# A one-core kernel of attention and two MoE layers: block 0 of the first layer in two halves around block 1

## The chip, the cores and the metric

The kernel runs on one core of a Trainium2 chip. The metric is the device time of one execution in microseconds (us); lower is better. Engines are named as in the profile: PE is TensorE (PEld its weight loads), DVE is VectorE, ACT is ScalarE, POOL is GpSimd, SP issues most DMAs. L546 is line 546 of the kernel before.

## The reference

```python
# q, k, v: (4, 8, 768, 64); sinks 4, window 128; x: 3072 tokens x 512
scores = np.where(is_sink | in_window, scale * q @ k.T, -1e9)
attn_out = softmax(scores) @ v
x = attn_out.transpose(0, 2, 1, 3).reshape(3072, 512)
h = np.maximum(x @ w_in, 0.0)          # w_in: 512 x 2048
x = (h * h) @ w_out                    # w_out: 2048 x 512
logits = x @ w_gate                    # 8 experts, the largest logit's one is taken
# for the tokens of each expert e:
h = np.maximum(x[mask] @ w1[e], 0.0)   # w1[e]: 512 x 1024
out[mask] = gate_w * eom[e] * (h @ w2[e])
```

Everything is fp32 in the reference. The kernel splits fp32 numbers into a high and a low half that PE takes (fp32r) and adds three products.

## The kernel before

The 3072 tokens are worked in 12 blocks of 256 (`NBLK`). Attention of block t writes its 256 tokens, transposed, into the one tile `xr`; `split_x(t)` (L507) then splits `xr` into `xT`, high and low halves, four pieces of 256 columns, the high half on ACT (L512) and the low half on DVE (L513). Each of the four needs its own part of `xr`; the branch in front of it (L509) is taken only for inputs of another kind.

The first layer of a block runs in 16 slices of the hidden width (`NF`). For slice j, `l1(t, j)` (L540) multiplies `xT` by `WI[j]` (12 matmuls of 256 columns, L546), takes the relu on ACT (L549), squares on DVE (L550; in block 0 every second slice on POOL), and splits the result into `h2` (ACT L552, DVE L553). `l2(t, j)` (L556) runs two slices later and adds `h2` times `WO[j]` (6 matmuls of 512 columns, L562) to two PSUM accumulators, psx0 and psx1. After slice 15 they are copied to a tile (L570 on ACT, L572 on DVE), from which `gate_pieces` (L584) works out the second layer's routing in four steps and stores the block to `x2tab` in DRAM.

The weights `WI` and `WO` arrive in 32 pieces of 512 KB (`conv`, L261): piece 2j is `WI[j]`, piece 2j + 1 is `WO[j]`. A piece is loaded into one of the three buffers of the ring `stage`, changed on ACT (L275, L276), put together on DVE by two shifts (L278, L279), cast into the high half (DVE L283, every third one ACT L281), and POOL subtracts to get the low half (L284). The main loop (L909 on) calls `cstep` in block 0 so that before slice j the pieces up to 17 + j are done in program order; 13 stand before slice 0.

The order of everything is made by a scheduler from the program's order and priorities, and each engine works its list in that order. Attention of block t is a list of timed events (`attn_events`, L515): two slots a slice, eight tiles (four pairs of heads, two halves of 128 queries), with `prep_k`, `prep_q`, `scores`, `ptrans`, `pv` at the leads of `LEADS`. In the kernel before the tiles of a block come every four slots, that is every two slices, so that attention of block t spreads over the 16 slices of block t - 1 and some of the block ahead. The last steps, `fin_sink` and `add_sink`, add the four sink tokens to `xr`. Blocks 0 and 1 do attention in plain fp32 (`T32`): a score tile is two matmuls in the program and four passes in the trace (L400), a product L472. From block 2 on they are split as the first layer is (L404, L479).

```python
            cstep(max(2 * j + 3, 17 + j) - st_["done"])
```

Of the kernel before, what the change touches and what calls it, by code (L numbers as in the profile page):

```python
# [30 lines left out]
XW = 513  # L31
# [3 lines left out]
LEADS = ((5, 2, 4.5, 8.5), (5, 2, 4.5, 8), (5.5, 2.5, 4.5, 8))  # L35
# [7 lines left out]
def kern(ctx, tc, q, k, v, n_sink, window, w_in, w_out, w_gate, w_og, w1, w2, out):  # L43
# [15 lines left out]
    xtab = dram.tile([B * H, D, S], F32, name="xtab")  # L59

# [446 lines left out]
    def split_x(t):  # L507
        b, u = divmod(t, NQ // 2)
        with tc.If(gv > 0):  # L509
            SY.dma_start(out=xr[:], in_=xtab[H * b:H * b + H, :, 256 * u:256 * u + 256].rearrange("(p e) d s -> (e d) p s", e=2))  # L510
        for kk in range(4):
            A.activation(out=xT[:, 0, kk], in_=xr[:, kk], func=AF.Copy)  # L512
            V.tensor_tensor(out=xT[:, 1, kk], in0=xr[:, kk], in1=xT[:, 0, kk].bitcast(F32), op=ALU.subtract)  # L513

    def attn_events(t):  # L515

        ev = []
        h0 = 32 * (t - 1) - 8
        a0, a1, a2, a3 = LEADS[min(t, 2)]
        for p in range(4):  # L520
            ev.append((h0 + 8 * p - a0, lambda p=p: prep_k(t, p)))
            ev.append((h0 + 8 * p - a1, lambda p=p: prep_q(t, p)))
        for n in range(8):
            ev.append((h0 + 4 * n, lambda n=n: scores(t, n // 2, n % 2)))
            ev.append((h0 + 4 * n + a2, lambda n=n: ptrans(t, n // 2, n % 2)))
            ev.append((h0 + 4 * n + a3, lambda n=n: pv(t, n // 2, n % 2)))
        if t % 3 == 0:
            ev.append((h0 + 31, lambda: prep_sink(t // 3)))
        else:
            ev.append((h0 + 31, lambda: fin_sink(t)))  # L530
# [9 lines left out]
    def l1(t, j):  # L540
# [9 lines left out]
        (G if t == 0 and j % 2 else V).tensor_tensor(out=hq[:], in0=hq[:], in1=hq[:], op=ALU.mult)  # L550
# [4 lines left out]

    def l2(t, j):  # L556
        if j == 0:
            acc[t] = [psX.tile([128, 512], F32, tag=f"x{m}", name=f"psx{m}") for m in range(2)]
        o = h2.pop((t, j))
        for m in range(2):  # L560
            for n, (a_, b_) in enumerate(((0, 0), (0, 1), (1, 0))):
                PE.matmul(acc[t][m][:], lhsT=o[:, a_, 128 * m:128 * m + 128], rhs=WO[j // 8][:, j % 8, b_, :],  # L562
                          start=(j == 0 and n == 0), stop=(j == NF - 1 and n == 2))
        if j == NF - 1:
            xs = []
            both = cv.tile([128, 2, XW], F32, tag="stage", name="x2s", bufs=3)
            for m in range(2):
                x = both[:, m]
                if m == 0:
# [338 lines left out]
    G2 = NBLK * NF  # L908
    for g in range(G2):  # L909
        t, j = divmod(g, NF)  # L910
# [20 lines left out]
        if t == 0:  # L931
            cstep(max(2 * j + 3, 17 + j) - st_["done"])
        with (tc.high_priority(20) if t == 0 else ExitStack()):
            swap = t > 0 and j == 0
            if swap:
                l2(*divmod(g - 2, NF))
# [3 lines left out]
            if j == NF - 1 and t + 1 < NBLK:  # L940
                split_x(t + 1)
            if swap:
                l1(t, j)
            elif g >= 2:
                l2(*divmod(g - 2, NF))
            if g >= 2:
                if j == 1 and t > 0:
                    gate_events(t - 1)
# [150 lines left out]
```

## Time and profile before

| | |
|---|---|
| runs | 1193.41 us median of 3 (1192.56 to 1198.88) |
| the profiled execution | 1196.3 us, its span 1194.5 us |
| PE busy | 1138.7 us (95% of the span) |
| DVE, ACT, POOL busy | 761.5, 626.5, 457.9 us |
| first layer's first l1 matmul | 59.50 us |

A row of a timeline gives its start, how long it lasted, engine, line, operation, what it writes and reads, how many instructions it merges, and in brackets the idle time of the engine before it with what ended that. A row of lines gives a group's count, its busy time and the mean length of one instruction, then the engine's idle time before its instructions. Granted clock is given as a share of 2.4 GHz; where no record of the clock lies in a stretch, it reads 1.00.

### The profile page before, as it was taken

What the parts mean: (1) busy time and instruction counts of PE and PEld (TensorE: products, weight loads), DVE (VectorE), ACT (ScalarE), POOL (GpSimd) and SP (SyncE); (2) the same over time, 40 slices, a digit from 0 to 9 for tenths busy, and PEclk for the clock granted to TensorE, in tenths of its full rate; (3) what the DMA queues carried; (4) which work ended last, traced back from release to release, by engine and by line L of the source; (5) the groups of instructions that cost most, each with busy time, mean ns of one, the idle gap of its engine ahead of it and who ended that gap; (6) DMA issues with size and microseconds to landing.
All of it is one profiled execution on the core that took longest, in us unless ns stands there. A gap on an engine that the chain in (4) does not pass through costs nothing. (4 is left out here: it accounts for less than half of the span.)

```text
span 1194.5 us, 24037 instructions
## 1 busy us (share of the span) xinstructions
PE 1138.7 (95%) x7022; PEld 945.7 (79%) x7022; DVE 761.5 (64%) x2123; ACT 626.5 (52%) x1740; POOL 457.9 (38%) x949
## 2 busy tenths in 40 slices
PE   4898889999999999999999999999899999999996
PEld 2476678888888888888888888887788888888884
DVE  4699776767676667676767677656611466764153
ACT  3677576767666766666676666545222222222200
POOL 4256665326565335555424556310211222222111
PEclk9999899999999999999999999999999999999998
DMA  4565411111211211121112120087411357554110
GB/s 123 132 181 176 137 35 45 32 51 37 54 32 28 50 37 46 35 49 29 47 35 51 37 54 1 19 182 207 133 39 44 100 179 255 189 203 151 42 51 23
DMA packets 139387, 100.08 MB, mean 84 GB/s; under 512 B 103903, under 2 KB 112223, under 8 KB 139234
## 3 DMA queue, kind: packets, MB, share of 16 engines
q1 hardware_dynamic: 132674, 83.85, 25.1%
q0 software_dynamic: 5472, 14.19, 3.6%
q8 instruction: 64, 1.05, 0.4%
q14 instruction: 89, 0.73, 0.3%
q10 hardware_dynamic: 1088, 0.26, 0.1%
HBM read 85.56 MB, written 13.76 MB: 83 GB/s over the span
## 5 line engine op out<-in xcount | busy, mean ns | idle before, releaser
L546 PE MATMUL psh<-xT,WI 128*128 128x256 f32 x2304 | 314.8, 285 | 10.6 <-POOL WI L284 8.1
L546 PEld LDWEIGHTS psh<-xT,WI 128*128 128x128 f32 x2304 | 294.9, 190 | 29.0 <-POOL WI L284 10.9
L867 PE MATMUL psh<-WI,xt 128*128 (+1 forms) x672 | 164.8, 400 | 0.3 <-ACT ht L847 0.3
L562 PE MATMUL psx<-WOb,h 128*128 128x512 f32 x576 | 157.8, 410 | 2.7 <-ACT h L552 2.4
L562 PE MATMUL psx<-WOa,h 128*128 128x512 f32 x576 | 159.0, 409 | 0.0
L867 PEld LDWEIGHTS psh<-WI,xt 128*128 128x128 f32 x672 | 124.3, 188 | 27.9 <-ACT xt L847 0.5
L550 DVE TENSOR_TENSOR r<-r 128x256 f32<-128x256 f32 x184 | 83.6, 455 | 68.3 <-ACT r L549 66.7
L562 PEld LDWEIGHTS psx<-WOb,h 128*128 128x128 f32 x576 | 102.6, 191 | 23.4 <-ACT h L552 3.9
L412 ACT ACTIVATE P<-P,st 128x260 f32<-128x260 f32 (+1 forms) x192 | 92.7, 485 | 47.4 <-DVE st L410 45.1
L883 DVE TENSOR_TENSOR ht<-psht,ht 128x512 fp32r<-128x512 f32 x56 | 38.5, 689 | 123.9 <-ACT ht L847 123.5
L549 ACT ACTIVATE r<-psh 128x256 f32<-128x256 f32 x192 | 72.2, 377 | 83.6 <-PE psh L546 72.4
L562 PEld LDWEIGHTS psx<-WOa,h 128*128 128x128 f32 x576 | 102.1, 190 | 17.4 <-issue 0.3
L553 DVE TENSOR_TENSOR h<-r,h 128x256 fp32r<-128x256 f32 x192 | 91.9, 479 | 29.3 <-ACT h L552 25.7
L905 POOL DMA_INDIRECT out_dram<-xg,pidx x28 | 31.2, 1116 | 193.5 <-ACT xg L904 152.0
L408 DVE CUSTOM_DVE_ANT_0 P<-pss,M 128x260 f32<-128x260 f32 (+1 forms) x184 | 72.5, 403 | 28.2 <-PE pss L404 14.3
L455 POOL TENSOR_SCALAR_AFFINE_SELECT PT<-PT 128x256 fp32r<-128x256 f32 x224 | 85.1, 415 | 12.9 <-DVE st L410 12.8
L552 ACT ACTIVATE h<-r 128x256 fp32r<-128x256 f32 x192 | 78.1, 408 | 22.2 <-DVE r L550 18.0
L896 PE MATMUL psy<-WOb,ht 128*128 (+1 forms) x336 | 85.1, 402 | 0.0
L896 PE MATMUL psy<-WOa,ht 128*128 (+1 forms) x336 | 84.1, 397 | 0.0
L873 ACT ACTIVATE r<-psh 128x512 f32<-128x512 f32 x48 | 28.7, 598 | 99.7 <-PE psh L867 97.8
L838 POOL DMA_INDIRECT xg<-x2tab,pidx x30 | 40.7, 1356 | 95.5 <-issue 55.9
L489 POOL TENSOR_TENSOR xr<-tB,tC 128x128 f32<-128x128 f32 x80 | 37.6, 470 | 97.8 <-DVE tB L488 95.3
(430 smaller groups left out, 1979.3 us busy)
## 6 DMA issues: line engine op xcount, KB each, us to landing
raw<-in_moe_w_dram SPq DMA_DIRECT2D x36, 1024.0 KB, 6.2
craw<-in_moe_w_in_dram SPq DMA_DIRECT2D x16, 512.0 KB, 3.8
craw<-in_moe_w_out_dram SPq DMA_DIRECT2D x16, 512.0 KB, 3.2
x2tab<-x2s SPq DMA_DIRECT2D x24, 256.5 KB, 3.1
kn<-in_k_dram SPq DMA_DIRECT2D x64, 96.0 KB, 2.3
vn<-in_v_dram SPq DMA_DIRECT2D x64, 96.0 KB, 2.2
qn<-in_q_dram SPq DMA_DIRECT2D x92, 64.0 KB, 2.1
kn<-in_k_dram SPq DMA_DIRECT2D x32, 64.0 KB, 2.1
```

The source lines that it names most:

```text
L408: V.tensor_tensor_reduce(out=P[:, e, 0:W], in0=ps[e][:, 0:W], in1=mask[:, 0:W], scale=1.0, scalar=-3.0e38, op0=ALU.add, op1=ALU.max, accum ...
L412: A.activation(out=P[:, e, 0:W], in_=P[:, e, 0:W], func=AF.Exp, scale=SCALE, bias=st[:, 2 + e:3 + e], accum_out=st[:, 4 + e:5 + e])
L455: G.affine_select(out=both[:, 1 - b, e], in_=bf[:, 0, e], pattern=[[0, 2], [1 - 2 * b, 128]], compare_op=ALU.is_gt if b else ALU.is_ge, fi ...
L546: PE.matmul(ps[:], lhsT=WI[:, j, a_, kk, :], rhs=x[:, b_, kk, :], start=(n == 0), stop=(n == 11))
L549: A.activation(out=hq[:], in_=ps[:], func=AF.Relu)
L550: (G if t == 0 and j % 2 else V).tensor_tensor(out=hq[:], in0=hq[:], in1=hq[:], op=ALU.mult)
L552: A.activation(out=o[:, 0], in_=hq[:], func=AF.Copy)
L553: V.tensor_tensor(out=o[:, 1], in0=hq[:], in1=o[:, 0].bitcast(F32), op=ALU.subtract)
L562: PE.matmul(acc[t][m][:], lhsT=o[:, a_, 128 * m:128 * m + 128], rhs=WO[j // 8][:, j % 8, b_, :], start=(j == 0 and n == 0), stop=(j == NF ...
L838: G.indirect_dma_start(out=x, out_offset=None, in_=x2tab[:] if s >= PRE else x2tab[0:256 * (NBLK - 3)], in_offset=bass.IndirectOffsetOnAxi ...
L867: PE.matmul(ps[:], lhsT=o[:, a_, kk, :], rhs=wview(n, par + 2048 * b_ + 512 * kk, 512), start=(c == 0), stop=(c == 11))
L896: PE.matmul(yp[s][:], lhsT=o[:, a_, kk, :], rhs=wview(2 + n, par + 2048 * b_ + 512 * kk, 512), start=(n == 0 and kk == 0 and c == 0), stop ...
```

## The change

The first layer now works block 0's slices 0 to 7, then all of block 1, then block 0's slices 8 to 15, then blocks 2 to 11 as before (`SEQ`). The input of block 0 is stored to DRAM (`x0d`) at the first split and loaded again three slices before it is needed; the sums over slices 0 to 7 are stored (`y0d`), loaded again at slice 13 of block 0 and added to the sums over slices 8 to 15. Both tiles come from the ring `stage`. Attention of block 1 takes two slots a tile instead of four, with leads of its own and its sink steps sooner. The weights' conversion asks for 15 + g pieces before step g of the new order (at least 2g + 3 in the first eight), up to step 23. Routing steps of block 1 come every four slots instead of eight. The squares of block 0's slices 8 to 15 all go to DVE.

```diff
-LEADS = ((5, 2, 4.5, 8.5), (5, 2, 4.5, 8), (5.5, 2.5, 4.5, 8))
+LEADS = ((5, 2, 4.5, 8.5), (5, 2, 3.9, 7.8), (5.5, 2.5, 4.5, 8))
+MID = NF // 2
+SEQ = [(0, j) for j in range(MID)] + [(1, j) for j in range(NF)] + [(0, j) for j in range(MID, NF)] + \
+      [(t, j) for t in range(2, NBLK) for j in range(NF)]
...
+        if t == 0:
+            SY.dma_start(out=x0d[:], in_=xr[:])
+        split(xr[:])
...
+        d = 2 if t == 1 else 4
...
-            ev.append((h0 + 4 * n, lambda n=n: scores(t, n // 2, n % 2)))
+            ev.append((h0 + d * n, lambda n=n: scores(t, n // 2, n % 2)))
...
+        elif t == 1:
+            ev.append((h0 + 18.5, lambda: fin_sink(t)))
+            ev.append((h0 + 20.5, lambda: add_sink(t, 0)))
+            ev.append((h0 + 22.5, lambda: add_sink(t, 1)))
...
-        (G if t == 0 and j % 2 else V).tensor_tensor(out=hq[:], in0=hq[:], in1=hq[:], op=ALU.mult)
+        (G if t == 0 and j < MID and j % 2 else V).tensor_tensor(out=hq[:], in0=hq[:], in1=hq[:], op=ALU.mult)
...
+        if t == 0 and j == NF - 3:
+
+            xout[0] = cv.tile([128, 2, XW], F32, tag="stage", name="x2s", bufs=3)
+            SY.dma_start(out=xout[0][:, :, 0:512], in_=y0d[:])
+        if t == 0 and j == MID - 1:
+            half = cv.tile([128, 2, XW], F32, tag="stage", name="y0", bufs=3)
+            A.activation(out=half[:, 0, 0:512], in_=acc[t][0][:], func=AF.Copy)
+            V.tensor_copy(out=half[:, 1, 0:512], in_=acc[t][1][:])
+            SY.dma_start(out=y0d[:], in_=half[:, :, 0:512])
...
+                if t == 0:
+                    V.tensor_tensor(out=x[:, 0:512], in0=acc[t][m][:], in1=x[:, 0:512], op=ALU.add)
...
-        if t == 0:
-            cstep(max(2 * j + 3, 17 + j) - st_["done"])
-        with (tc.high_priority(20) if t == 0 else ExitStack()):
+        if g < 3 * MID:
+            cstep(max(2 * g + 3 if g < MID else 0, 15 + g) - st_["done"])
+        if g == 3 * MID - 3:
+            x0 = cv.tile([128, 2 * XW], F32, tag="stage", name="x0", bufs=3)
+            x0 = x0[:, 0:1024].rearrange("p (k c) -> p k c", k=4)
+            SY.dma_start(out=x0, in_=x0d[:])
+        with (tc.high_priority(20) if g < MID else ExitStack()):
...
-            if j == NF - 1 and t + 1 < NBLK:
-                split_x(t + 1)
+            if last_of(t, j) and g + 1 < len(SEQ):
+                if (t, j) == (1, NF - 1):
+                    split(x0)
+                else:
+                    split_x(SEQ[g + 1][0])
```

How the instructions stand. Lines of the changed kernel are further down in the file: l1 is L562 there (L546 before), l2 L584 (L562), a score tile L406 (L400), a transposed tile L445 (L439), a product L478 (L472), the branch of `split_x` L515 (L509); on DVE the shifts are L284 and L285 (L278, L279), the cast L289 (L283), the square L566 (L550), the split of h L569 (L553), the split of `xT` L524 (L513).

PE at the start of block 0's slices, from the branch on, before:

```order
L509 COMPARE_AND_BRANCH
L509 UNCONDITIONAL_BRANCH x2
L400 MATMUL pss_1183<-kT,qT 128x260
L400 MATMUL pss_1184<-kT,qT 128x260
L439 MATMUL pspt<-ident,P 128x128 x4
L546 MATMUL psh<-xT,WI 128x256 x2
L472 MATMUL pso<-PT_1092,vn 64x128 x4
L439 MATMUL pspt<-ident,P 128x128 x3
L546 MATMUL psh<-xT,WI 128x256 x6
L439 MATMUL pspt<-ident,P 128x128
L546 MATMUL psh<-xT,WI 128x256 x6
```

and in the changed kernel:

```order
L515 COMPARE_AND_BRANCH
L515 UNCONDITIONAL_BRANCH x2
L445 MATMUL pspt<-ident,P 128x128 x4
L562 MATMUL psh<-xT,WI 128x256 x6
L445 MATMUL pspt<-ident,P 128x128
L406 MATMUL pss_1165<-kT,qT 128x260
L445 MATMUL pspt<-ident,P 128x128 x2
L406 MATMUL pss_1166<-kT,qT 128x260
L445 MATMUL pspt<-ident,P 128x128
L478 MATMUL pso<-PT_1110,vn 64x128 x4
L562 MATMUL psh<-xT,WI 128x256 x6
L406 MATMUL pss_1250<-kT,qT 128x260
```

The score tile that stood behind the branch (pss_1183) now stands ahead of it, and the one after it comes within the first l1 matmuls.

PE at the first border, the end of block 0's slices (psx_1398 and psx_1399 are their accumulators) and the start of block 1's, in the changed kernel:

```order
L502 MATMUL psst<-ident,psk_118 128x128
L584 MATMUL psx_1399<-WOa,h_1640 128x512 x3
L510 MATMUL pso_1600<-pskT,vsk 128x256 x2
L325 MATMUL psk__1723<-ident,kn 128x128 x3
L478 MATMUL pso<-PT_1527,vn 64x128 x4
L510 MATMUL pso_1643<-pskT,vsk 128x256 x2
L325 MATMUL psk__1913<-ident,kn 128x128 x3
L515 COMPARE_AND_BRANCH
L515 UNCONDITIONAL_BRANCH x2
L351 MATMUL psq<-ident,qn 128x128 x2
L562 MATMUL psh<-xT,WI 128x256 x36
L584 MATMUL psx_1769<-WOa,h_1693 128x512 x3
```

The last product (L478) and the sink products (L510) of block 1's attention stand directly ahead of the branch, and three whole l1 of block 1 follow it.

DVE around the last cast of a weight, before:

```order
L278 SCALAR_TENSOR_TENSOR fbuf<-craw 128x512
L408 ISA P,st<-pss_1949,M_109 128x260
L408 ISA st 128x1
L279 SCALAR_TENSOR_TENSOR fbuf<-craw,fbuf 128x512
L410 TENSOR_SCALAR st<-st 128x2
L357 TENSOR_TENSOR qT<-psq,qT 128x256
L283 CAST WOb<-fbuf 128x512
L505 TENSOR_TENSOR xr<-pso_2032,xr 128x512
```

and in the changed kernel:

```order
L566 TENSOR_TENSOR r<-r 128x256
L414 ISA P,st<-pss_2087,M_111 128x260
L414 ISA st 128x1
L414 ISA P,st<-pss_2088,M_111 128x260
L414 ISA st 128x1
L284 SCALAR_TENSOR_TENSOR fbuf<-craw 128x512
L569 TENSOR_TENSOR h_2071<-r,h_2071 128x256
L416 TENSOR_SCALAR st<-st 128x2
L285 SCALAR_TENSOR_TENSOR fbuf<-craw,fbuf 128x512
L289 CAST WOb<-fbuf 128x512
```

Before, the last cast stands ahead of block 0's last sink add and before the split of block 1's input. Now it stands in block 1, behind the square of that block's ninth l1 (r of the first row; h_2071 is the split of the eighth).

## Rows read from the trace of the kernel before

**Rows 1.** Table of stretches: us, then busy us and count by engine, granted clock.

```profile
61.00:131.80 70.80, 61.53 (x342) 45.04 (x339) 69.93 (x136) 49.63 (x118) 47.15 (x55) 0.98 0.62 184
131.80:142.00 10.20, 10.20 (x32) 6.64 (x31) 4.44 (x11) 3.08 (x8) 4.08 (x6) 0.50 0.44 127
142.00:152.90 10.90, 9.59 (x60) 7.29 (x60) 10.75 (x24) 7.25 (x20) 7.29 (x11) 1.00 0.28 64
152.90:221.50 68.60, 66.56 (x486) 58.10 (x486) 48.91 (x177) 48.84 (x154) 37.76 (x90) 1.00 0.13 33
221.50:283.50 62.00, 61.51 (x441) 53.20 (x440) 42.81 (x149) 42.61 (x133) 23.33 (x53) 1.00 0.18 44
```

**Rows 2.** Timeline of DVE at the borders of block 0.

```profile
60.97 0.42 DVE L513 TENSOR_TENSOR xT<-xr,xT 128x256 fp32r<-128x256 f32 x1
...
152.50 0.41 DVE L283 CAST WOb<-fbuf 128x512 fp32r<-128x512 f32 x1
...
155.92 2.05 DVE L513 TENSOR_TENSOR xT<-xr,xT 128x256 fp32r<-128x256 f32 x4
```

**Rows 3.** Lines of DVE, 61 to 152.9 us: count, busy us, mean ns.

```profile
L278 DVE SCALAR_TENSOR_TENSOR fbuf<-craw 128x512 int32<-128x512 int32 x25 | 23.7, 948 | 4.2 <-ACT craw L276 3.4 <-POOL V L364 0.7 <-POOL psk L427 0.2
L279 DVE SCALAR_TENSOR_TENSOR fbuf<-craw,fbuf 128x512 int32<-128x512 int32 x26 | 21.1, 812 | 0.0
L553 DVE TENSOR_TENSOR h<-r,h 128x256 fp32r<-128x256 f32 x15 | 10.3, 688 | 0.0
L422 DVE TENSOR_SCALAR P<-P,st 128x260 f32<-128x260 f32 x12 | 7.0, 605 | 0.0
...
L550 DVE TENSOR_TENSOR r<-r 128x256 f32<-128x256 f32 x8 | 4.8, 605 | 0.1
...
L513 DVE TENSOR_TENSOR xT<-xr,xT 128x256 fp32r<-128x256 f32 x4 | 2.7, 685 | 0.0
```

**Rows 4.** Single lines: shortest, median and longest ns; first and last start.

```profile
L278 DVE SCALAR_TENSOR_TENSOR fbuf<-craw x32: 676/684/1766, 13.9 to 149.5; 128x512 int32<-128x512 int32 x32
...
L553 DVE TENSOR_TENSOR h<-r,h x184: 395/426/1492, 69.8 to 797.9; 128x256 fp32r<-128x256 f32 x184
```

**Rows 5.** Lines of POOL, 60 to 153 us: the low halves.

```profile
L284 POOL TENSOR_TENSOR WI<-fbuf,WI 128x512 fp32r<-128x512 f32 x13 | 19.8, 1522 | 7.5 <-DVE WI L283 7.2 <-ACT WI L281 0.2
```

**Rows 6.** Waits, 60 to 160 us: total us, times, longest.

```profile
PE psh L546 <- POOL WI L284: 8.1, 8, 2.3
```

**Rows 7.** Timeline of PE, late in block 0.

```profile
119.88 0.66 PE L472 MATMUL pso<-PT,vn 128*64 128x128 f32 x8
...
131.42 1.58 PE L546 MATMUL psh<-xT,WI 128*128 128x256 f32 x7 [2.26 <-POOL WI L284]
...
137.45 3.35 PE L562 MATMUL psx<-WOb,h 128*128 128x512 f32 x7
...
144.52 0.66 PE L439 MATMUL pspt<-ident,P 128*128 128x128 f32 x4
```

**Rows 8.** Timeline of PE, around the first l1 matmuls.

```profile
43.62 0.90 PE L319 MATMUL psk__948<-ident,kn 128*128 128x128 f32 x3 [0.69 <-ACT PT L443]
...
56.84 1.24 PE L400 MATMUL pss<-kT,qT 64*128 64x260 f32 x4
...
64.68 1.45 PE L546 MATMUL psh<-xT,WI 128*128 128x256 f32 x10
...
71.13 0.71 PE L400 MATMUL pss<-kT,qT 64*128 64x260 f32 x4
```

**Rows 9.** Timeline of PE in a settled block.

```profile
345.67 1.63 PE L562 MATMUL psx<-WOb,h 128*128 128x512 f32 x6
347.14 1.57 PE L546 MATMUL psh<-xT,WI 128*128 128x256 f32 x12
...
349.11 0.63 PE L404 MATMUL pss<-kT,qT 64*128 64x260 f32 x6
```

**Rows 10.** DMA issues: count, KB each, median us from issue to landing.

```profile
craw<-in_moe_w_out_dram SPq DMA_DIRECT2D x16, 512.0 KB, 3.2
```

More of the change, by code (lines that the diff above doesn't have):

```diff
@@ L59, in kern @@
     xtab = dram.tile([B * H, D, S], F32, name="xtab")
+    x0d = dram.tile([128, 4, 256], F32, name="x0d")
+    y0d = dram.tile([128, 2, 512], F32, name="y0d")
     ident = const.tile([128, 128], F32, name="ident")
@@ L510, in split_x, with split @@
             SY.dma_start(out=xr[:], in_=xtab[H * b:H * b + H, :, 256 * u:256 * u + 256].rearrange("(p e) d s -> (e d) p s", e=2))
+        if t == 0:
+            SY.dma_start(out=x0d[:], in_=xr[:])
+        split(xr[:])
+    def split(x):
         for kk in range(4):
-            A.activation(out=xT[:, 0, kk], in_=xr[:, kk], func=AF.Copy)
-            V.tensor_tensor(out=xT[:, 1, kk], in0=xr[:, kk], in1=xT[:, 0, kk].bitcast(F32), op=ALU.subtract)
+            A.activation(out=xT[:, 0, kk], in_=x[:, kk], func=AF.Copy)
+            V.tensor_tensor(out=xT[:, 1, kk], in0=x[:, kk], in1=xT[:, 0, kk].bitcast(F32), op=ALU.subtract)
     def attn_events(t):
@@ L554, in l1, with first_of, last_of @@
         h2[t, j] = o
+    def first_of(t, j):
+        return j == 0 or t == 0 and j == MID
+    def last_of(t, j):
+        return j == NF - 1 or t == 0 and j == MID - 1
     def l2(t, j):
-        if j == 0:
+        if first_of(t, j):
             acc[t] = [psX.tile([128, 512], F32, tag=f"x{m}", name=f"psx{m}") for m in range(2)]
@@ L562, in l2 @@
                 PE.matmul(acc[t][m][:], lhsT=o[:, a_, 128 * m:128 * m + 128], rhs=WO[j // 8][:, j % 8, b_, :],
-                          start=(j == 0 and n == 0), stop=(j == NF - 1 and n == 2))
+                          start=(first_of(t, j) and n == 0), stop=(last_of(t, j) and n == 2))
+        if t == 0 and j == NF - 3:
[6 more added lines that the diff above has]
+            SY.dma_start(out=y0d[:], in_=half[:, :, 0:512])
         if j == NF - 1:
             xs = []
-            both = cv.tile([128, 2, XW], F32, tag="stage", name="x2s", bufs=3)
+            both = xout[0] if t == 0 else cv.tile([128, 2, XW], F32, tag="stage", name="x2s", bufs=3)
             for m in range(2):
                 x = both[:, m]
-                if m == 0:
+                if t == 0:
+                    V.tensor_tensor(out=x[:, 0:512], in0=acc[t][m][:], in1=x[:, 0:512], op=ALU.add)
+                elif m == 0:
                     A.activation(out=x[:, 0:512], in_=acc[t][m][:], func=AF.Copy)
@@ L778, in run_to, with gate_events @@
                 f()
-    def gate_events(t):
+    def gate_events(t, h0):
         g = gate_pieces(t)
-        h0 = 32 * (t + 1)
-        for o, f in zip((4, 8, 12, 16) if t == NBLK - 2 else (6, 14, 22, 30), g):
+        for o, f in zip((4, 8, 12, 16) if t in (1, NBLK - 2) else (6, 14, 22, 30), g):
             events.append((h0 + o, f))
@@ L906, in m_l2 @@
                                  in_=y, in_offset=None, bounds_check=NT - 1, oob_is_err=False)
-    G2 = NBLK * NF
-    for g in range(G2):
-        t, j = divmod(g, NF)
+    for g, (t, j) in enumerate(SEQ):
         if t == NBLK - 2 and j == 8:
@@ L930, in kern @@
             load_raw(pc, es[half + 1], True)
-        if t == 0:
-            cstep(max(2 * j + 3, 17 + j) - st_["done"])
-        with (tc.high_priority(20) if t == 0 else ExitStack()):
-            swap = t > 0 and j == 0
+        if g < 3 * MID:
[5 more added lines that the diff above has]
+        with (tc.high_priority(20) if g < MID else ExitStack()):
+            swap = g > 0 and first_of(t, j)
             if swap:
-                l2(*divmod(g - 2, NF))
+                l2(*SEQ[g - 2])
             else:
@@ L944, in kern @@
             elif g >= 2:
[L945 to L948, printed above, removed]
+                l2(*SEQ[g - 2])
+            if g >= 2 and SEQ[g - 2][1] == NF - 1:
+                gate_events(SEQ[g - 2][0], 2 * (g - 1))
             run_to(2 * g + 1.9)
```

8 lines of the change are left out of this document (4 added, 4 removed).

## The prediction

> **What bounds the kernel now.** I read the table of stretches first [rows 1]. From 221.5 to 283.5 us, one whole block of the first layer, PE is busy 61.5 of 62.0 us and DVE 42.8: PE is the bound there, and stays so in the blocks that follow. From 61.0 to 131.8 us it is the other way round: DVE is busy 69.9 of 70.8 us, PE 61.5 with waits inside. The excess is in block 0. Its input split begins on DVE at 60.97 us, the last cast of a weight at 152.50 and block 1's input split at 155.92 [rows 2]: 95 us from split to split, where a settled block takes 62. So the change can win or lose where DVE is the bound, up to the last weight conversion, done at 152.9 us; after that PE has hardly a hole.
>
> Within that stretch I read DVE by line [rows 3]. 25 weight conversions (the shifts L278 and L279, and a cast) take over half of DVE's 85.1 us (69.9 + 4.4 + 10.8 [rows 1]). Instructions are stretched there: L278 averages 948 ns and its shortest is 676, L553 688 against 395 [rows 3, 4]. In the same time POOL subtracts the low halves, at 1.5 us each [rows 5]; I take the stretching to go with their number. The waits name the other loss: PE stood 8.1 us, eight times, for POOL's low half of a weight [rows 6], since conversions run only a little ahead of the slice that needs them. After the longest of these waits the granted clock is 0.50, from 131.8 us on [rows 1]: seven l1 matmuls take 1.58 us and seven l2 matmuls 3.35 [rows 7], where ten l1 took 1.45 [rows 8], and DVE, waiting on PE, idles 5.8 of 10.2 us [rows 1].
>
> **The change part by part.** The sum is made against the profiled execution, 1196.3 us with a span of 1194.5; the median of the three runs, 1193.41, lies 2.9 below it, and the sum's difference is put on that median.
>
> *Start of block 0.* Block 1's attention moves up, so PE now issues, ahead of the last product of block 0's attention, two more q transposes, three more k transposes and one more pair of score matmuls. At the pace before 60 us that is 0.6, 0.8 and 1.2 us (43.62 and 56.84 [rows 8]; two transposes as two thirds of three): 2.6 if all lies on the path, nothing if it fits into PE's short waits there. I take 2, since PE had work nearly all that time.
>
> *DVE up to the last conversion.* I counted its instructions between the first split of xT and the last cast in both orders. The 17 casts are the same. Added: one pair of shifts (0.68 each), two h splits and five squares (0.40 each; these squares came after the last cast or from POOL), four xT splits for block 1 (0.41, of the same size), one copy of half sums and one more sink add (0.7 each, the size of a shift), two mask passes, two scalings and five small ones (2.1 together); one copy of k and one of q go (1.0). At shortest lengths [rows 4], with 0.07 us of overlap off each, that is 7.4 us; at the means of the stretch [rows 3] 12.9. POOL's low halves grow by one at most, so the lower end is nearer: 8. DVE's way to the last conversion is thus longer, not shorter: conversions are as many, and more attention and more slices stand before the last.
>
> *DVE's idle time on that way.* Before: 60.97 to 152.9 is 91.9 us, less 85.1 busy, so 6.8. PE's waits for weights go, because block 1 reuses the weights of slices 0 to 7 while the rest are converted. Low bound 1.2 us, the rate of the first 70.8 us; high bound 13 (rival 2). I take 4, nearer the low end: the waits for weights go, but slices 0 to 7 are dense with attention, and what DVE waits for there comes from PE. That is -2.8. A row bears on this: a score tile took 1.24 us at 56.84, where PE had long been busy with fp32 attention, and 0.71 at 71.13, after dense l1 matmuls [rows 8]; so attention alone ran at half clock, 1.2 GHz. The Trainium skill, "TensorE: Matmul & The Clock Gate", section "What's actually happening", says that the throttled state is the default and that activity of PE releases it. By that rule slices 0 to 7, where PE always has attention queued, run at 2.4 GHz, DVE idles the low bound, and the sum is 2.8 us lower; the row speaks against relying on it for this kind of work, and the 4 us stay.
>
> *PE after the last conversion.* Before, 68.6 us pass from 152.9 to 221.5, of which PE is busy 66.6 [rows 1]. In the new order, at DVE's last cast, PE stands two l1 slices (18 against 16), one l2 slice (16 against 15), one score tile and one pair of transposes further. Twelve l1 matmuls take 1.5 us, six l2 1.47 from one start to the next, a score tile 0.6 [rows 9], two transposes 0.2: 5.2 us less to do.
>
> *What goes through DRAM.* The inputs and the half sums are 512 KB each, stored once and reloaded once; a load of 512 KB took 3.2 us from issue to landing [rows 10]. The inputs' store must land before block 1's attention writes xr; the first such write stands on ACT behind three of the four splits, which the new order spreads over some 13 us. Each reload is issued two to three slices (7 to 11 us) before its use; that covers it. Cost 0; if the cover is gone, one load, 4 us. The third block border copies half sums out of psx, one copy on ACT and one on DVE (counted above), while PE has the next block's l1, as at the borders before: 0. Block 1's router steps come every two slices instead of four, beside slices that PE bounds: 0.
>
> Sum: 2 + 8 - 2.8 - 5.2 = **+2.0 us**. 1193.4 + 2.0 gives **1195.4 us**, inside half a per cent (6 us), which is about what a measurement of this kernel can tell from no change.
>
> **Rivals.**
> 1. *PE sets the pace from the border on: faster.* If the start costs nothing, DVE idles 1.2 us and its added work is 7.4, the sum is 0 + 7.4 - 5.6 - 5.2 = -3.4. Beyond that, DVE's work from block 1's input split to the last cast is 39 us at the means of rows 3 and 27 at the shortest lengths, 33 between, against 29 of PE (ten l1, eight l2, three score tiles, two us of transposes). Should conversions stop holding anything up there, another 4 us go: 1186 us. For it: no slice of that stretch needs a weight that is still to come. Against it: DVE's order is fixed, with shifts between the squares, so no slice can pass a conversion.
> 2. *PE falls to half clock in slices 0 to 7: slower.* All of block 1's attention now ends within eight slices. PE's work there is 8 x (1.5 + 1.47) plus some six tiles at 0.71 + 0.66 + 0.66 (scores, products, transposes [rows 7, 8]), 36 us, in 57 to 60 us of DVE. At half clock it is 72, and PE becomes the bound: it decides as soon as over six tenths of that work run at half clock. The likeliest places are the first 15 us, where DVE does attention between the splits of xT (PE has 10 us of work, at half clock 20: +5), the last 20, after the last l1 (11, at half clock 22: +2), and the first slices of block 1 (+2). With +9 the time is 1204 us. For it: until 59.5 us PE was busy nearly all the time with fp32 attention, yet at half clock: a score tile took 1.24 us at 56.84 and 0.71 at 71.13, with the rise between them, after dense l1 matmuls had begun [rows 8]. Against it: from 61.0 to 131.8 us the clock was 0.98 though PE waited [rows 1].
> 3. *A reload is late.* That of the half sums waits for a buffer that block 1's router steps hold. One load exposed: 2 + 4, 1199.4 us.
>
> **How the numbers follow.** Forecast 0.42 (its own range 1189 to 1201), rival 1 0.25, rival 2 0.27, rival 3 0.06. Faster by over 0.5% is rival 1 and a little of the forecast's lower end: 0.26. Slower is rival 2 and most of rival 3's upper half: 0.31. The rest, 0.43, is within. The range takes in both rivals and the bounds of the start and the idle time: 1185 to 1206.
>
> **What would show it.** Right: the first split of xT lies near 63 us and block 1's near 123, DVE busy over 95% between them; no l1 matmul waits for a low half of POOL; the last cast of a weight comes 4 to 9 us later than 152.50, with PE two slices further; then no holes on PE. Wrong: a last cast before 152.50 means that I priced DVE too high (rival 1); a granted clock of 0.50 for over 10 us between 65 and 125 us is rival 2; an evacuation of psx that waits for a DMA is rival 3. A gain of over 12 us would mean that DVE was not the bound at all.

## The result and the profile after

The changed kernel takes 1205.21 us (median of 12 runs, 1198.84 to 1208.04), the kernel before 1193.64 in the runs beside it. The medians differ by 11.6 us where the forecast had 2.0; the ratio, worked out over all runs, is 1.0086 (95% interval 1.0066 to 1.0106), that is 10.3 us. The profiled execution took 1204.69 us, its span is 1202.8; it lies 0.5 us below its median, and that of the kernel before 2.7 above its own, so between the two traces there are 8.4 us to find. In all traces below I follow two marks: the first split of `xT` and the first relu of block 2. From there to block 10's first relu the two kernels differ by 0.8 us.

The table of stretches, kernel before, from the first split to its last cast's end, from there to block 2's first relu, and both together (us from and to, length, busy us and count of PE, PEld, DVE, ACT and POOL, granted clock, DMA share, GB/s):

```profile
60.97:152.93 91.96, 81.38 (x429) 59.03 (x426) 85.16 (x170) 60.03 (x144) 58.55 (x72) 0.93 0.56 164
152.93:220.70 67.77, 65.73 (x479) 57.27 (x478) 48.25 (x173) 48.25 (x153) 37.76 (x90) 1.00 0.13 33
60.97:220.70 159.73, 147.11 (x906) 116.30 (x903) 133.40 (x343) 108.28 (x296) 96.31 (x162) 0.96 0.38 108
```

The same stretches of the changed kernel, and one piece of the second:

```profile
60.35:157.82 97.47, 85.11 (x476) 65.20 (x474) 92.29 (x192) 68.60 (x165) 57.23 (x72) 0.89 0.58 173
157.82:226.60 68.78, 63.25 (x429) 54.04 (x430) 45.52 (x161) 44.24 (x141) 33.36 (x85) 0.95 0.15 39
...
160.60:167.40 6.80, 6.80 (x24) 5.32 (x23) 3.44 (x11) 2.08 (x7) 4.23 (x14) 0.50 0.00 0
...
60.35:226.60 166.25, 148.37 (x905) 119.24 (x904) 137.81 (x353) 112.84 (x304) 90.59 (x157) 0.91 0.40 118
```

Read by the forecast's own terms, the first relu of block 2 comes 226.60 - 220.70 = 5.90 us later. The first split is 0.62 sooner. DVE up to the last cast is busy 92.29 - 85.16 = 7.13 longer. Its idle time there is 5.18 (97.47 - 92.29) instead of 6.80: 1.62 less. What follows the last cast takes 68.78 instead of 67.77: 1.01 more, where 5.2 less was forecast. These are -0.62 + 7.13 - 1.62 + 1.01 = 5.90. The last term is the one that failed. In it PE does have less to do, 63.25 us against 65.73, though 6.80 of the 63.25 ran at a granted clock of 0.50 (1.2 GHz) and would have taken some 3.4 at full clock (an estimate, half of 6.80): 5.9 us less work, near the 5.2 forecast. But PE idles 5.53 us there instead of 2.04, and the clock costs the 3.4.

The timeline of the changed kernel at that hole: PE, ACT, POOL and DVE (start, us, engine, line, operation; in brackets the idle time before and what ended it):

```profile
156.09 1.09 PE L562 MATMUL psh<-xT,WI 128*128 128x256 f32 x8
160.38 0.49 PE L445 MATMUL pspt<-ident,P 128*128 128x128 f32 x2 [3.20 <-DVE PT L457]
160.55 1.17 PE L562 MATMUL psh<-xT,WI 128*128 128x256 f32 x4
```

```profile
157.86 0.36 ACT L565 ACTIVATE r<-psh 128x256 f32<-128x256 f32 x1
159.19 0.38 ACT L456 ACTIVATE PT<-pspt 128x256 fp32r<-128x256 f32 x1 [0.97 <-POOL WOb L290]
```

```profile
157.89 1.26 POOL L290 TENSOR_TENSOR WOb<-fbuf,WOb 128x512 fp32r<-128x512 f32 x1 [2.10 <-DVE WOb L289]
```

```profile
157.39 0.43 DVE L289 CAST WOb<-fbuf 128x512 fp32r<-128x512 f32 x1
157.98 1.20 DVE L420 TENSOR_SCALAR st<-st 128x2 f32<-128x2 f32 x1 [0.17 <-ACT P L418]
159.09 0.41 DVE L424 TENSOR_TENSOR P<-P 128x256 f32<-128x256 f32 x1
159.43 0.15 DVE L421 RECIPROCAL st<-st 128x2 f32<-128x2 f32 x1
159.50 0.40 DVE L566 TENSOR_TENSOR r<-r 128x256 f32<-128x256 f32 x1
159.82 0.41 DVE L457 TENSOR_TENSOR PT<-pspt,PT 128x256 fp32r<-128x256 f32 x1
```

PE stops in the middle of an l1 (8 of 12 matmuls), because the transposes of block 2's attention stand there and the one psT bank still holds the transposed tile before them. That bank is read by ACT (L456) and DVE (L457) into the tile `PT`, and ACT's copy waits for POOL's low half of a weight. Attention has no use for that weight. The link is in the line of the allocation:

```python
    fbuf = att.tile([128, 2, 512], F32, tag="PT", name="fbuf", bufs=1)
```

The conversions' `fbuf` and attention's `PT` (from block 2 on) share one buffer, so the first `PT` must wait until POOL has read `fbuf` for the last time, at 159.15. That wait is not the whole hole. What ended it was DVE's part of `PT` (L457), and from 157.98 on DVE worked without a pause until then: with this order of DVE's list, ACT's copy coming 0.97 us sooner would not have moved L457. The shared buffer shows in the list itself: `PT` can't be written before the last conversion is out of `fbuf`, so L457 stands behind the last cast. L420, beside POOL's low half, took 1.20 us (its median in the first 300 us is 0.17). In the kernel before ACT's wait was there too, and short:

```profile
154.30 0.38 ACT L450 ACTIVATE PT<-pspt 128x256 fp32r<-128x256 f32 x1 [0.27 <-POOL WOb L284]
```

Block 2's first tile stands at the same step in both orders, while the conversions, 15 + g instead of 17 + j, end two steps later. The forecast followed the queues on that way, and not this buffer.

The other thing that stands out is the start. The splits of `xT` on DVE, changed kernel:

```profile
60.35 0.42 DVE L524 TENSOR_TENSOR xT<-xr,xT 128x256 fp32r<-128x256 f32 x1 [0.42 <-ACT xT L523]
...
62.76 0.41 DVE L524 TENSOR_TENSOR xT<-xr,xT 128x256 fp32r<-128x256 f32 x1
...
70.97 0.41 DVE L524 TENSOR_TENSOR xT<-xr,xT 128x256 fp32r<-128x256 f32 x1
...
71.64 0.41 DVE L524 TENSOR_TENSOR xT<-xr,xT 128x256 fp32r<-128x256 f32 x1
```

The four are 11.3 us apart and were 3.9, from 60.97 [rows 2] to 64.90, since DVE now does block 1's attention, and weight shifts between its pieces, between the second and the third. So the first slice is done late, first relu changed and before:

```profile
75.09 0.64 ACT L565 ACTIVATE r<-psh 128x256 f32<-128x256 f32 x2
```

```profile
65.93 0.66 ACT L549 ACTIVATE r<-psh 128x256 f32<-128x256 f32 x2 [0.30 <-PE psh L546]
```

That is 9.2 us, and between 65 and 125 us the granted clock was 0.50 from 68.4 to 75.2, from 95.7 to 99.1 and from 119.6 on, 15.6 us in all. Rival 2 named just this as its mark, and its time, 1204, is nearly what was measured. Three accounts thus had to be told apart: the hole behind the last conversion (H), DVE's added work whatever its place (D, the sum's second term), and the start with the clock (S, rival 2); beside them the traffic through DRAM (rival 3).

### The profile page after: what moved, and what is told of

Its sections match the earlier page's. It is cut to its first block, busy times and chain, and to the rows that moved or that the text cites. A ratio compares the mean times of both kernels' runs of the same rounds, so it can differ in the third digit from the quotient of the medians.

```text
span 1202.8 us, 24063 instructions
## 1 busy us (share of the span) xinstructions
PE 1140.7 (95%) x7022; PEld 948.9 (79%) x7022; DVE 765.3 (64%) x2133; ACT 628.0 (52%) x1744; POOL 452.6 (38%) x945
## 5 line engine op out<-in xcount | busy, mean ns | idle before, releaser
L562 PE MATMUL psh<-xT,WI 128*128 128x256 f32 x2304 | 313.3, 285 | 3.5 <-DVE WI L289 1.0
L562 PEld LDWEIGHTS psh<-xT,WI 128*128 128x128 f32 x2304 | 296.7, 191 | 16.0 <-issue 1.5
L584 PE MATMUL psx<-WOa,h 128*128 128x512 f32 x576 | 162.4, 413 | 1.1 <-DVE h L569 0.7
L584 PE MATMUL psx<-WOb,h 128*128 128x512 f32 x576 | 155.7, 408 | 1.3 <-issue 0.5
L566 DVE TENSOR_TENSOR r<-r 128x256 f32<-128x256 f32 x188 | 85.9, 457 | 69.2 <-ACT r L565 66.6
L584 PEld LDWEIGHTS psx<-WOb,h 128*128 128x128 f32 x576 | 102.2, 190 | 21.7 <-ACT h L568 1.5
L584 PEld LDWEIGHTS psx<-WOa,h 128*128 128x128 f32 x576 | 102.4, 192 | 21.1 <-DVE h L569 1.8
L569 DVE TENSOR_TENSOR h<-r,h 128x256 fp32r<-128x256 f32 x192 | 93.6, 488 | 31.4 <-ACT h L568 28.4
L461 POOL TENSOR_SCALAR_AFFINE_SELECT PT<-PT 128x256 fp32r<-128x256 f32 x224 | 84.8, 413 | 13.0 <-DVE st L416 11.6
```

The costliest lines, as they stand in the source:

```text
L461: G.affine_select(out=both[:, 1 - b, e], in_=bf[:, 0, e], pattern=[[0, 2], [1 - 2 * b, 128]], compare_op=ALU.is_gt if b else ALU.is_ge, fi ...
L562: PE.matmul(ps[:], lhsT=WI[:, j, a_, kk, :], rhs=x[:, b_, kk, :], start=(n == 0), stop=(n == 11))
L566: (G if t == 0 and j < MID and j % 2 else V).tensor_tensor(out=hq[:], in0=hq[:], in1=hq[:], op=ALU.mult)
L569: V.tensor_tensor(out=o[:, 1], in0=hq[:], in1=o[:, 0].bitcast(F32), op=ALU.subtract)
```

## The experiments

Twelve kernels; ratios are to the kernel before, run beside each.

| kernel | median us | ratio | 95% interval |
|---|---|---|---|
| changed kernel | 1205.21 | 1.0086 | 1.0066 to 1.0106 |
| a_fbuf: last pieces in a buffer of their own | 1198.22 | 1.0036 | 1.0018 to 1.0054 |
| a_pace: conversions two steps sooner | 1202.76 | 1.0055 | 1.0034 to 1.0075 |
| a_dbl: DRAM transfers doubled | 1202.24 | 1.0065 | 1.0041 to 1.0089 |
| a_nodram: DRAM transfers left out | 1217.29 | 1.0189 | 1.0164 to 1.0215 |
| b_dense: before, dense attention | 1199.07 | 1.0031 | 1.0012 to 1.0050 |
| a_mid10: a_fbuf, split after slice 10 | 1197.64 | 1.0026 | 1.0009 to 1.0043 |
| a_lowdve: all low halves on DVE | 1198.19 | 1.0027 | 1.0011 to 1.0043 |
| a_fbuf_low13: a_fbuf, 19 low halves on DVE | 1197.42 | 1.0018 | 0.9996 to 1.0041 |
| b_low13: before, 19 low halves on DVE | 1195.76 | 1.0013 | 0.9996 to 1.0029 |
| a_mid10_low13 | 1195.73 | 1.0007 | 0.9993 to 1.0021 |
| a_mid12_low13 | 1193.86 | 0.9986 | 0.9969 to 1.0002 |
| a_mid12_sink | 1195.05 | 1.0018 | 1.0002 to 1.0034 |

### a_fbuf: is it the shared buffer?

```diff
+    fend = att.tile([128, 512], F32, name="fend", bufs=1)
...
-            f, fi = fbuf[:, c % 2], fbuf[:, c % 2].bitcast(I32)
+            f = fend[:] if c > 28 else fbuf[:, c % 2]
+            fi = f.bitcast(I32)
```

> The changed kernel, with the last three conversions (pieces 29 to 31) put together in a 2 KB tile of their own instead of the buffer that they share with PT, so that block 2's first PT need not wait for POOL's low half of the last piece. Theory H (holes): in the changed kernel PE stood 3.20 us at 160.38 for PT (L457), whose copy on ACT had waited for POOL's low half L290, and the granted clock was 0.50 from 160.6 to 167.4, in which PE did some 3.4 us worth of work in 6.8: with the hole gone both go, 1.0086 becomes 1.003 to 1.005 of before (1197 to 1200 us). Rival D (DVE): the time goes with DVE's longer way to the last cast, 4.9 us later than in the kernel before; then PE merely waits elsewhere, and it stays at 1.007 to 1.010. Rival C (clock alone): the hole goes, but the clock falls there all the same; 1.006.

It is: 1205.2 became 1198.2, inside H's range and outside D's. The first copy into `PT` now comes at 148.70 and waits for nothing, and DVE's part of it stands ahead of the last two casts (150.81 and 160.30) instead of behind them (ACT, DVE and PE, timelines of a_fbuf):

```profile
148.70 0.39 ACT L458 ACTIVATE PT<-pspt 128x256 fp32r<-128x256 f32 x1
```

```profile
149.34 0.41 DVE L459 TENSOR_TENSOR PT<-pspt,PT 128x256 fp32r<-128x256 f32 x1
```

```profile
152.56 0.86 PE L487 MATMUL pso<-PT,V 128*128 128x256 f32 x4 [1.64 <-POOL PT L463]
...
157.10 1.57 PE L564 MATMUL psh<-xT,WI 128*128 128x256 f32 x12
158.51 0.49 PE L327 MATMUL psk__2152<-ident,kn 128*128 128x128 f32 x3
158.76 1.64 PE L586 MATMUL psx<-WOa,h 128*128 128x512 f32 x6
160.23 1.57 PE L564 MATMUL psh<-xT,WI 128*128 128x256 f32 x12
```

A smaller hole, 1.64 us, comes in its place at 152.56, with 3.4 us of clock 0.50 behind it instead of 6.8; from 157.10 to 161.64 l1 and l2 follow each other without a gap. Up to 143 us the two traces are the same within 0.5 us, so the earlier holes and half clocks, all still there, are not in these 7 us. That D's last cast came later still, at 160.3, and the time fell, speaks against D as the account of these 7 us. The edit frees the buffer and with it the order of the lists; the runs don't separate the wait from the order. Nor do the two traces have all 7 us at this place: block 2's first relu comes 4.2 us sooner (222.4, 226.6), block 10's 4.9, and 2.8 of the 7.7 us between the two spans lie behind that.

### a_pace: the same wait, undone by the other road

```diff
-            cstep(max(2 * g + 3 if g < MID else 0, 15 + g) - st_["done"])
+            cstep(max(2 * g + 3 if g < MID else 0, 17 + g) - st_["done"])
```

> The changed kernel with 17 + g pieces asked for before step g instead of 15 + g, as in the kernel before, so that the conversions end two steps sooner; fbuf and PT share their buffer as they did. Theory H: block 2's first PT stands at the same step, and the last piece is now out of the buffer before it; the hole of 3.20 us and the half clock behind it go by this road too, 1.002 to 1.006 of before. If the conversions' lateness has no part in it (rival D, DVE's work alone): 1.007 to 1.010.

1.0055 is inside H's range, but its interval reaches into D's range and into that of the changed kernel, so this run decides nothing. The edit also puts two more conversions ahead of the first slice, whose relu comes at 79.8 us in its trace (75.1). The profiled execution took 1209.4 us, the longest of its six, so its trace is not typical; in it PE waited 0.5 us for DVE's `PT`, and 2.9 us near 155 for ACT's `P` (L430).

### a_dbl and a_nodram: the traffic through DRAM

a_dbl repeats each of the four `SY.dma_start` lines. a_nodram takes them out:

```diff
-        if t == 0:
-            SY.dma_start(out=x0d[:], in_=xr[:])
...
-            SY.dma_start(out=xout[0][:, :, 0:512], in_=y0d[:])
...
-            SY.dma_start(out=y0d[:], in_=half[:, :, 0:512])
...
-                    V.tensor_tensor(out=x[:, 0:512], in0=acc[t][m][:], in1=x[:, 0:512], op=ALU.add)
...
-            SY.dma_start(out=x0, in_=x0d[:])
...
-                    split(x0)
+                    split(xr[:])
```

> The changed kernel with each of its four transfers through DRAM made twice. A second load of the same tile lands some 3 to 4 us after the first. If the detour is covered (the forecast's 0): within 1.5 us of the changed kernel, 1.007 to 1.010 of before. If a transfer lies on the path (rival 3): 3 to 8 us more, 1.011 to 1.016.

> The changed kernel without its traffic through DRAM: block 0's input is neither stored nor loaded again (the second split reads xr as it stands), the half sums are copied out and dropped, and the last sums are copied instead of added; four transfers of 512 KB and two buffers of the ring less, and block 0 is wrong. If the detour costs nothing, as the forecast had it: 0 to -1.5 us against the changed kernel (ratio to before 1.007 to 1.009). If a transfer or a buffer holds something up (rival 3): 3 to 5 us less, 1.004 to 1.006.

Twice the traffic costs nothing that can be measured (1.0065 lies a little under the range expected for a covered detour, and its interval overlaps that of the changed kernel): rival 3 falls, the forecast's 0 holds. a_nodram met neither of its ranges and can't be read by its total: its block 0 is wrong, which can change the router's choice for those tokens (not followed), and from block 10's first relu to the end it took 491.9 us where the changed kernel took 478.6. Up to there it gives no sign of a gain either: block 2's first relu at 228.9 (226.6), and PE's hole for `PT` is there as before, 4.10 us at 163.30.

### b_dense: what block 1's dense attention costs by itself

```diff
-LEADS = ((5, 2, 4.5, 8.5), (5, 2, 4.5, 8), (5.5, 2.5, 4.5, 8))
+LEADS = ((5, 2, 4.5, 8.5), (5, 2, 3.9, 7.8), (5.5, 2.5, 4.5, 8))
...
+        d = 2 if t == 1 else 4
...
-            ev.append((h0 + 4 * n, lambda n=n: scores(t, n // 2, n % 2)))
+            ev.append((h0 + d * n, lambda n=n: scores(t, n // 2, n % 2)))
...
+        elif t == 1:
+            ev.append((h0 + 18.5, lambda: fin_sink(t)))
```

> The kernel before, in its order of slices, with block 1's attention alone made as dense as in the change (two slots a tile, its leads, its sink steps at 18.5 to 22.5). If the denser attention is what costs (more fp32 attention at the start, DVE's attention work ahead of the early slices): first slices later, 1.004 to 1.009 of before. If it costs no more than the 2 us that the forecast gave the start: 0.999 to 1.003, since block 0's later slices get the DVE time back.

1.0031 lies between the two expectations, and its interval reaches into both. The first relu came at 78.9 us, 13 later than in the kernel before, but block 2's at 225.9, only 5.2 later: most of a late start is given back. So by its ratio the density costs about 1193.6 x 0.0031 = 3.7 us in the old order of slices, and a_fbuf, which has that density and the new order without the hole, is at 1.0036. The new order by itself is then worth nothing that these runs resolve (intervals of 0.2% on either side). Of the 10.3 us of the ratio 1.0086, about 3.7 go with the density and 6.0 (1.0086 - 1.0036) with the buffer, each known to some 2 to 3 us.

### a_mid10: is the start, or the clock in it, what is left?

```diff
-MID = NF // 2
+MID = 10
...
+        h0 += 4 * (t == 1)
...
-        if g < 3 * MID:
+        if g < 24:
...
-        if g == 3 * MID - 3:
+        if g == MID + NF - 3:
```

> The kernel of a_fbuf (1.0036 of before), with block 0 split after slice 10 instead of 8 and block 1's attention four slots later, as dense as in the change, so that two of its tiles stand ahead of the first slice instead of four. Theory S (start): in the changed kernel the first slice's relu came at 75.1 us and at 65.9 in the kernel before, because DVE does block 1's attention between the second and the third input split (62.8 and 71.0 us); with that undone the splits lie within 4 us again, the first relu comes near 66, and 4 to 8 us go: 0.996 to 1.000 of before. Rival P (price moved, not gone): DVE is the bound up to the last cast whatever the order, the attention is done later instead, and the time stays at 1.002 to 1.005.

Rival P came out: 1.0026, inside its range and not below a_fbuf's interval. The start was mended in part (first relu at 69.5, a_fbuf 74.7), and the clock with it, as the table of stretches from first split to block 2's first relu shows (a_mid10, then a_fbuf):

```profile
61.10:221.80 160.70, 143.65 (x905) 115.81 (x905) 136.63 (x348) 108.92 (x299) 97.92 (x160) 0.97 0.40 116
```

```profile
60.00:222.40 162.40, 146.09 (x905) 117.83 (x904) 136.75 (x353) 113.26 (x305) 91.89 (x157) 0.92 0.41 120
```

DVE's busy time is the same in both, 136.63 and 136.75. The granted clock was 0.97 against 0.92, with 10.2 us at 0.50 instead of 25.0, and block 2's first relu comes 0.6 us sooner (221.8, 222.4). So rival 2's mechanism was seen, and no price of it shows in this pair: up to the last cast DVE set the pace, and PE at half clock waited less. The pair differs in order too, so it is not a test of the clock alone. Behind the last cast, where PE was busy without a pause, 6.8 us at half clock are put at their half, 3.4, in the sum above. a_mid10 also has a hole of 2.89 us at 158.05 that ends with DVE's `PT`, though no conversion of its last pieces uses that buffer: late work on DVE can make such a hole without the sharing.

### Low halves on DVE: a_lowdve, a_fbuf_low13, b_low13

```diff
-            G.tensor_tensor(out=lo, in0=f, in1=hi.bitcast(F32), op=ALU.subtract)
+            (V if c > 12 else G).tensor_tensor(out=lo, in0=f, in1=hi.bitcast(F32), op=ALU.subtract)
```

(a_lowdve puts V for every piece.)

> The changed kernel with the weights' low halves (L290) on DVE instead of POOL. In the kernel before DVE's instructions were stretched by some 0.89 us for each of POOL's low halves; on DVE a low half should take about 0.7 (the shifts' shortest length, same size). If the stretching is the price of POOL's work beside DVE, DVE's way to the last cast gets no longer (26 x (0.7 - 0.89) = -5 us) and no slice waits for POOL: -2 to -6 us against the changed kernel, 1.004 to 1.007 of before. If DVE's instructions keep their lengths, DVE has 18 us more to do up to the last cast and the time is 1.015 to 1.025.

> The kernel of a_fbuf with the low halves of pieces 13 to 31 on DVE. With all low halves on DVE the changed kernel had its first relu at 83.8 us, 8.7 later, and yet came out 7 us faster: from the first relu to block 2's it took 136.5 us instead of 151.5. If that shorter stretch is the price of POOL's low halves beside DVE, the start stays at 75 and the stretch is 137 to 141: 5 to 9 us below a_fbuf, 0.996 to 0.999 of before. If it was the two pieces of work changing places (the half clock before 84 us, conversions done ahead), it is 1.002 to 1.005 of before.

> The kernel before, with the low halves of pieces 13 to 31 (those converted beside the slices) on DVE instead of POOL. DVE gets 19 instructions of 0.7 us and loses 19 stretches of 0.89 if each of POOL's low halves stretches it so: -3.6 us on DVE, and PE's waits for POOL's low halves (8.1 us in eight waits) shrink: 0.993 to 0.998 of before. If the stretching is not POOL's, DVE has 13 us more to do: 1.005 to 1.011.

On DVE itself the price is as expected. Lines of b_low13, from the first split to 149.1 us, in the last low half (count, busy us, mean ns):

```profile
L278 DVE SCALAR_TENSOR_TENSOR fbuf<-craw 128x512 int32<-128x512 int32 x25 | 19.3, 773 | 4.7 <-ACT craw L276 4.6
L279 DVE SCALAR_TENSOR_TENSOR fbuf<-craw,fbuf 128x512 int32<-128x512 int32 x26 | 18.2, 701 | 0.0
L553 DVE TENSOR_TENSOR h<-r,h 128x256 fp32r<-128x256 f32 x16 | 8.8, 547 | 0.1
L284 DVE TENSOR_TENSOR WOb<-fbuf,WOb 128x512 fp32r<-128x512 f32 x8 | 6.2, 779 | 0.0
...
L284 DVE TENSOR_TENSOR WI<-fbuf,WI 128x512 fp32r<-128x512 f32 x9 | 6.2, 684 | 0.0
```

The shifts take 773 and 701 ns instead of 948 and 812 [rows 3], and though DVE has 19 low halves more, 12.4 us of them in the two rows here, it is busy 79.9 us up to there, where the kernel before has 85.2 up to its last cast; the last cast itself begins at 147.6 instead of 152.5. The time did not follow, against the expectation: 1.0013, block 2's first relu at 221.5 (220.7). What was won on DVE is lost behind that, where PE now needs 72.40 us instead of 67.77 (b_low13, table of stretches):

```profile
61.60:149.10 87.50, 77.13 (x430) 58.06 (x426) 79.92 (x183) 58.82 (x142) 31.78 (x49) 0.94 0.56 167
149.10:221.50 72.40, 69.16 (x476) 59.18 (x477) 50.37 (x180) 48.86 (x154) 36.87 (x95) 0.98 0.15 36
```

PE was the next bound, close behind DVE: up to the last cast of the kernel before DVE is busy 85.2 us and PE 81.4. a_lowdve missed its range by 1.6 us on the good side (1198.2, 1.0027; its interval reaches in). Stretching need not be all of it: PE has no wait over 0.9 us for `PT` or `P` between 140 and 180 us, so the hole went here too, with the buffer shared as before, while its late start (first relu at 83.8) is given back. The two remedies overlap: a_fbuf_low13, with both, is at 1.0018, and can't be told from a_fbuf; from first relu to block 2's it took 142.9 us, short of the 137 to 141 expected.

### Is there a version below both?

a_mid10_low13 joins the edits of a_mid10 and of the 19 low halves. a_mid12_low13 splits after slice 12 with three slots a tile:

```diff
-MID = NF // 2
+MID = 12
...
-        d = 2 if t == 1 else 4
+        d = 3 if t == 1 else 4
+        h0 += 2 * (t == 1)
...
-            ev.append((h0 + 18.5, lambda: fin_sink(t)))
-            ev.append((h0 + 20.5, lambda: add_sink(t, 0)))
-            ev.append((h0 + 22.5, lambda: add_sink(t, 1)))
+            ev.append((h0 + 25.5, lambda: fin_sink(t)))
+            ev.append((h0 + 27.5, lambda: add_sink(t, 0)))
+            ev.append((h0 + 29.5, lambda: add_sink(t, 1)))
```

a_mid12_sink is the same with `h0 + 28.85` in the last line; at 29.5 the second sink sum of block 1 came behind the split that reads it, so a_mid12_low13 leaves two of block 1's four pairs of heads without their sink terms.

> The kernel of a_mid10 (1.0026 of before) with the low halves of pieces 13 to 31 on DVE. From the first relu to block 2's, a_fbuf took 147.7 us and with the low halves on DVE 142.9; if that gain of some 4 us holds with the earlier start of a_mid10 (first relu at 69.5 instead of 75), block 2's first relu comes at 214 to 218 and the time is 0.994 to 0.999 of before: a version below both. If DVE's work up to the last cast is the bound and the gain was the late start given back, it stays at 1.000 to 1.003.

> As a_mid10_low13, but block 0 is split after slice 12 and block 1's attention takes three slots a tile, the first tile at slot -6. Less dense attention, fewer slices left for after block 1. If density is what costs (holes of PE over 1 us, with half clock behind them): fewer of them, and 0.992 to 0.998 of before. If what counts is how many slices run ahead of their weights, this is nearer to the kernel before: 0.999 to 1.002.

> As a_mid12_low13, with block 1's second sink sum ahead of the input split that needs it (there it came behind the split, and block 1 lacked it), so half a slot more is waited for at block 1's start. If the gain there (0.9986 of before) belongs to the order and not to the sum that was left out: 0.997 to 1.001 of before. If the missing sum had hidden a wait at the border: 1.001 to 1.004.

a_mid10_low13, at 1.0007, met its second expectation: the earlier start brought nothing that the time shows, though block 2's first relu came at 218.2 us in its trace, at the edge of what the first expectation named. a_mid12_low13 fell between its two, and a_mid12_sink came out in its second range (1.0018), with an interval that reaches into both. No version is below the kernel before by more than its interval. a_mid12_sink is the telling one: block 2's first relu came at 213.7 us, 7.0 sooner than in the kernel before, block 10's at 714.1, 3.3 sooner, and the medians are 1195.05 and 1193.98. Half of what is won at the start is gone by block 10, where two of PE's holes between 210 and 230 us (0.69 and 0.89) end with DVE's `x2U`, a router step of block 0 or 1; where the rest goes lies within the spread of single executions (6.5 us among its twelve), and was not followed further.

## Why the prediction was right, and where it was wrong

**The range held, the centre did not.** 1205.2 lies within 1185 to 1206, at its slow end, beside rival 2's 1204; the forecast's own 1195.4 is 9.8 us off, and the change is slower by more than the half per cent to which the likeliest case was put. That the range held was in part luck: its slow end was made for rival 2, and the hole that put the time there stood in no rival.

**Start, +2.** Mis-sized as a delay. Its upper bound is 2.7 by the rows named, not 2.6 (three k transposes took 0.90). The first split came 0.6 us sooner, not 2 later, but the first slice 9.2 later, since the work moved up sits between the splits. The prediction said that the splits spread over some 13 us (11.3) and drew nothing from it for the first slice. Behind it DVE goes on with other work of the same path, and most of it is given back (in b_dense 13 us at the first relu are 5.2 at block 2's).

**DVE up to the last conversion, +8.** Right: 7.1 us more, and the last cast 4.9 us later, within the 4 to 9 named. The lower prices were the right end. Block 1's split, forecast near 123, began at 121.97; DVE was busy 57.68 of the 61.62 us between, 94% and not over 95.

**DVE's idle time, -2.8.** Right in sign, 1.6 less. PE's waits for weights did not all go: one l1 waited 1.01 us for DVE's high half, at 94.43, and 0.82 for POOL's low half, at 96.07.

**PE after the last conversion, -5.2.** This step failed, as "then no holes on PE". The work was less by the size forecast (5.9), but PE stood 3.5 us longer, and the clock then cost some 3.4. a_fbuf shows the cause, the buffer that `fbuf` and `PT` share: 7.0 us by the medians, 6.0 by the ratios, 4.2 in the traces up to block 2's first relu. That 3.5 and 3.4 add up to nearly 7 is no proof, since a_fbuf has a smaller hole and 3.4 us of half clock in their place. The order of DVE quoted ahead of the prediction ends at the last cast, and the first `PT` stands behind it; ACT's wait of 0.27 us in the trace of before was the one sign that the two are tied.

**DRAM, 0.** Right; a_dbl bears it out.

**Rival 1** (PE sets the pace from the border on) had the start at nothing (-0.6) and DVE's added work at 7.4 (7.1), and both came; it falls by DVE's idle time, 5.2 us and not 1.2, and by the hole. Its further 4 us rest on 29 us of PE work, which by its own terms is 15 + 11.8 + 1.8 + 2 = 30.6. **Rival 2** gave the right time by the wrong road: its mark was met, 15.6 us at half clock between 65 and 125, and a_mid10, which has 10.2 us at half clock where a_fbuf has 25.0, is not faster by anything that shows. The half clock that the sum above charges is the one behind the hole, from 160.6 on.

The row that was weighed against the page of the Trainium skill "TensorE: Matmul & The Clock Gate" (section "What's actually happening", activity of PE releases the throttled state) was on the whole the better guide for attention alone. Table of stretches, a_lowdve, where the first slices come late (the last column but two is the granted clock):

```profile
43.30:50.10 6.80, 5.67 (x28) 3.04 (x28) 5.94 (x23) 5.42 (x14) 0.84 (x4) 1.00 0.74 188
50.10:66.20 16.10, 14.11 (x48) 7.85 (x47) 10.19 (x35) 9.72 (x28) 4.12 (x14) 0.50 0.54 162
50.10:84.20 34.10, 23.64 (x92) 14.93 (x91) 25.28 (x63) 19.27 (x46) 4.20 (x14) 0.50 0.63 193
84.20:120.00 35.80, 33.89 (x200) 24.55 (x199) 30.94 (x83) 27.14 (x69) 15.24 (x28) 1.00 0.48 144
```

From 43.3 to 50.1 us PE has fp32 attention alone and the clock is 1.00. From 50.1 to 66.2 it has attention and two l1 matmuls, and the clock is 0.50 though PE is busy for 14.11 of 16.10 us. It stays there up to 84.2, but in that part PE also stands 5.91 and 2.09 us waiting for `xT`, and 22 more l1 matmuls run; from 84.2 on, with the slices, it is 1.00. The trace doesn't contradict the Trainium skill, but shows that attention of this kind can't be counted on for full clock, as the forecast had it.

What stays open: 1.6 us between block 10 and the end of the two traces (478.6 and 477.0), where the changed kernel has 3.4 us at clock 0.50 from 860.3 on and the kernel before none; ten of the fourteen traces of this study have such a record, beginning between 849 and 862 us, whatever their edit. a_fbuf's has none, and takes 475.8 us there: this may be part of the 2.8 us by which it gains behind block 10.

## What to carry to other kernels

When a phase is moved later, list not only the queues that it passes but every buffer that its tiles share by tag with a later phase: the wait appears on an engine and a line that have nothing to do with it, and a wait of 0.3 us in the old trace was the warning here. The second bound can lie close behind the first: time saved on DVE up to the last cast was lost again on PE behind it (b_low13). Of a stretch at half clock, ask first whether TensorE sets the pace in it; where DVE did, these traces show no price.

## What the hardware showed that was not expected

POOL's low halves stretch DVE one by one. In the changed kernel one ran from 138.38 to 139.68, and beside it a DVE subtraction whose shortest length is 395 ns [rows 4] took 1.39 us:

```profile
138.56 1.39 DVE L569 TENSOR_TENSOR h<-r,h 128x256 fp32r<-128x256 f32 x1
```

```profile
138.38 1.30 POOL L290 TENSOR_TENSOR WI<-fbuf,WI 128x512 fp32r<-128x512 f32 x1 [0.70 <-DVE WI L289]
```

Its end, 139.95, lies 0.27 us behind POOL's, as if it had stood until POOL was done. The Trainium skill, "SBUF — State Buffer", section "Who interferes with whom", says that the only contention is over the port pair that the two engines share, an exclusive lock, and that a DVE instruction with two SBUF inputs contends with a POOL instruction that reads SBUF. The trace agrees, and a_lowdve shows the other side: from 84 to 157 us, without low halves on POOL, the same subtraction averages 418 ns and the shifts 693 and 683. b_low13 shows that such a price can be taken off DVE without the time following.

Holes of PE shorter than the stretches at half clock stood ahead of them in the changed kernel (each named by its length and the time at which PE went on): 1.01 us at 94.43, then 0.50 from 95.7 to 99.1; 1.21 at 117.71, then 0.50 from 119.6 to 126.4; 1.98 at 143.35, then 0.50 from 143.5 to 146.9; 3.20 at 160.38, then 0.50 to 167.4. But not every hole has one: in the kernel before a hole of 1.57 us at 155.59 had none behind it. What decides between them is open.
